# Linear attention into a snake MLP on one core: the order of the opening's loads, casts and copies, and of the second batch's preparation

## The chip, the cores and the metric

The kernel runs on one NeuronCore of a Trainium2 chip. The metric is the device time of one execution in microseconds (us). Five engines work side by side, each in its own program order: TensorE (PE, with its weight loads as PEld), VectorE (DVE), ScalarE (ACT), GpSimd (POOL) and SyncE (SP). SP, ACT and POOL also issue DMA transfers, each on a queue of its own; POOL's transfers here also cast float32 to bfloat16 on the way.

## The reference

q, k and v are float32 of 8 batches x 8 heads x 576 tokens x 64. Then a two-layer network with a periodic activation works on the 4608 tokens of 512 channels:

```python
q_s = softmax of q over its 64 channels
k_s = softmax of k over the 576 tokens
kv  = einsum('bhsd,bhse->bhde', k_s, v)
x   = einsum('bhsd,bhde->bhse', q_s, kv)        # (batch, token) x (head, channel)
h   = x @ w_in                                   # 512 -> 2048
g   = h + sin(alpha * h)**2 / (alpha + 1e-9)     # alpha: one number per hidden column
out = g @ w_out                                  # 2048 -> 512
```

## The kernel before, in words

**Tiling.** The tokens are worked off in nine blocks t of 512. The hidden layer of a block is 16 *slots* ni of 128 columns; a slot is four matmuls (`mm_h`, L261) over the four 128-row blocks of w_in in the order 0, 2, 1, 3, then a sine on ACT (L267), a square on ACT, POOL or DVE (L269, L271, L273) and a combine on DVE into g (`combine`, L277). The output of a block is four column groups of 16 matmuls each (`mm_o`, L281). A batch of tokens is split by head pairs into two halves `ii` (0 and 1). For each half the kernel does: exp of q and k on ACT, the sums and the division of q on DVE and POOL, eight transposes of q on PE (L199), the k-v product on PE (`kv_mm`, 36 small matmuls, L172), its normalization on DVE (`kv_norm`, L182), and four matmuls of q with it (`attn_x`, L216). These give two of the four row blocks of xT: half 0 gives blocks 0 and 2, half 1 gives 1 and 3.

**What sets the order.** The schedule is written by hand: every engine executes its instructions in the order of the code, and `take(os, n)` puts the next n output matmuls of the block before between other steps of PE. Semaphore waits follow from the data. A DMA is issued when its queue's engine reaches it. To hold an issue back, the code puts a one-element copy ahead of it: `GP_CP(held, ...)` on POOL waits until a load has landed, and a `DVE_CP` of a zero into the target of a load makes SP wait until DVE has come that far.

**The opening.** SP loads halves of batch 0: q, k, q, v, k (L309). ACT's queue loads alpha as 16 rows of 128 (L311); PE transposes it with the identity (L327), and DVE copies it to `alpha_sb` and takes the reciprocal (L328, L329). POOL waits for k's first half (L338), issues v's second half in two parts and then w_in by columns: 0 to 255 for row blocks 0 and 2, the same columns for 1 and 3, and then 256 columns at a time for all four row blocks up to 1023, later 512 at a time (L107), then w_out's first eight blocks of 128 rows (L110). DVE and POOL cast the two parts of v's second half (L335). xT of half 0 and the transposed q of half 1 are copied out of PSUM by DVE and ACT (L395 to L397); ACT loads its sine table at L398. PE then does the first two row blocks of slots 0 and 1, the attention matmuls of half 1, and the first two row blocks of slots 2 and 3. xT of half 1 is copied twice by DVE (L407).

**Block 0 and batch 1.** During the slots of block 0, the table `late` (L457) issues loads after certain slots: q of batch 1, first half, after slot 6; w_out blocks 8 to 11 after slot 8 and 12 to 13 after slot 10, on POOL; q's second half and all of k and v of batch 1 after slot 13, on SP. In the output of block 0 (`o_quad`) hidden blocks 12 to 15 come last: matmuls 49 to 56 need blocks 12 and 13, the last eight need 14 and 15. 46 output matmuls are followed by the steps of batch 1 with output matmuls between them (L486 to L512). POOL issues w_out blocks 14 and 15 once k of batch 1 has landed (L471, L472).

Of the kernel before, what the change touches and what calls it, by code (L numbers as in the profile page):

```python
# [23 lines left out]
def kernel(  # L24
# [14 lines left out]
    nc = tc.nc  # L39
# [7 lines left out]
    nN = d_ff // 128  # L47
# [58 lines left out]
    def load_win(c0, c1, cc=slice(0, 4)):  # L106
        nc.gpsimd.dma_start(out=win[:, cc, c0:c1], in_=win_v[:, cc, c0:c1])  # L107

    def load_wout(n0, n1):
        nc.gpsimd.dma_start(out=wout[:, n0:n1, :], in_=wout_v[:, n0:n1, :])  # L110


    A = {}
# [48 lines left out]
    def kv_mm(b, ii, pool, split=False):  # L162

        if ii == 0 or split:
            A["kvp", b] = pool.tile([128, 2, 512], F32, name="kvp", tag="a")
        kvp, ke, vt = A["kvp", b], A["ke", b], vb[b % 2]
        for j in range(J):
            for x in range(2):
                h = 2 * ii + x
                for e in range(2):  # L170
                    r = slice(64 * e, 64 * e + 64)
                    nc.tensor.matmul(kvp[64 * x:64 * x + 64, e, ii * 65:(ii + 1) * 65],  # L172
                                     ke[r, j, h * 64:(h + 1) * 64],
                                     vt[r, j, h * 65:(h + 1) * 65],
                                     start=(j == 0), stop=(j == J - 1))

    def kv_norm(b, i0=0, i1=2):

        kt, m = kbd[b % 2], i1 - i0
        kvr = small.tile([128, 2, 2], F32, name="kvr")[:, :, 0:m]  # L180
        src = A["kvp", b][:, :, i0 * 65:i1 * 65].rearrange("p e (ii c) -> p e ii c", ii=m)
        nc.vector.reciprocal(kvr, src[:, :, :, D])  # L182
        nc.vector.tensor_tensor(kt[:, :, i0:i1], src[:, :, :, 0:D],
                                kvr.unsqueeze(3).to_broadcast([128, 2, m, D]), op=ALU.mult)
# [123 lines left out]

    for n, t, ii in (("q", q, 0), ("k", k, 0), ("q", q, 1), ("v", v, 0), ("k", k, 1)):  # L309
        load0(nc.sync, n, t, ii, 0, 8 if n == "q" else J)  # L310
    nc.scalar.dma_start(out=alpha_rows, in_=moe_alpha.rearrange("(no ni) -> no ni", ni=128))  # L311
    make_identity(nc, ident)
    DVE_CP(identb, ident)
    zero = singles.tile([128, 1], F32, name="zero")
# [8 lines left out]

    tp0 = ps_h[0].tile([128, 8, 128], BF16, name="tp", tag="a")
    warm = ps_h[0].tile([128, 4, 128], F32, name="warm", tag="a")
    tpa = warm[:, 0, 0:nN]
    nc.tensor.transpose(tpa, alpha_rows, ident[0:nN, 0:nN])  # L327
    DVE_CP(alpha_sb, tpa)  # L328
    nc.vector.reciprocal(inva_sb, alpha_sb)  # L329

    def cast_v0(ii, j0, j1, eng):
        vv = vb[0].rearrange("p j (i c) -> p i j c", i=4)
        eng(vv[:, 2 * ii:2 * ii + 2, j0:j1, 0:D], staged["v", 0][:, ii::2, j0:j1])  # L335
# [2 lines left out]
    GP_CP(held, staged["k", 0][:, 0, 0, 0:1])  # L338
    load0(GP, "v", v, 1, 0, 5)
    load0(GP, "v", v, 1, 5, 9)  # L340
    for ii in range(2):
        load_win(0, 256, slice(ii, 4, 2))
    for c in range(1, 4):
        load_win(256 * c, 256 * c + 256)

    def warm_up(n):
# [36 lines left out]
    kv_norm(0, 0, 1)  # L383
    tp1 = ps_l.tile([128, 8, 128], BF16, name="tp", tag="l")
    q_transpose_ii(0, 1, 0, 8, tp1)
    cast_v0(1, 0, 5, DVE_CP)
    cast_v0(1, 5, 9, GP_CP)
    for c in range(2, 4):
        load_win(512 * c, 512 * c + 512)
# [2 lines left out]

    xp = [bank("b") for _ in range(2)]
    attn_x(0, 0, 0, 8, xp)
    DVE_CP(xT[:, 0, 0:MF], xp[0])  # L395
    ACT_CP(xT[:, 2, 0:MF], xp[1])
    ACT_CP(A["qT", 0][:, 1, 0:8], tp1)  # L397
    nc.scalar.activation(zero, zero, AX.Sin)  # L398
    kv_mm(0, 1, ps_k, split=True)
    kv_norm(0, 1, 2)  # L400
    for ki in range(2):
        for ni in range(2):
            mm_h(0, ni, ki, ki + 1)
    xp = [bank("l") for _ in range(2)]
    attn_x(0, 1, 0, 8, xp)
    for x in range(2):
        DVE_CP(xT[:, 2 * x + 1, 0:MF], xp[x])  # L407
    for ki in range(2):
        for ni in range(2, 4):
            mm_h(0, ni, ki, ki + 1)  # L410

    def h_slot(t, ni, sq, lag):
        hp = mm_h(t, ni, 2 if ni < (4, 1, 0)[min(t, 2)] else 0)
# [18 lines left out]
    def take(it, n=1000):  # L432
        for _ in range(n):
            if next(it, 0) == 0:
                return
# [4 lines left out]
    with ES:  # L440
        def load_q1(ii):
            if ii == 0:
                staged["q", 1] = stage.tile([128, 4, J, D], F32, name="st_q", tag="st")
            st = staged["q", 1]
            DVE_CP(st[:, ii, 0, 0:1], zero)
            nc.sync.dma_start(out=st[:, ii::2, 0:8].rearrange("p i j d -> p i (j d)"),
                              in_=src_view(q, 1)[:, ii::2, 0:8 * D])

        def load_kv1():
            for n in "kv":  # L450
                staged[n, 1] = stage.tile([128, 4, J, D], F32, name=f"st_{n}", tag="st")
            for ii in range(2):
                for n, t in (("k", k), ("v", v)):
                    nc.sync.dma_start(out=staged[n, 1][:, ii::2].rearrange("p i j d -> p i (j d)"),
                                      in_=src_view(t, 1)[:, ii::2])

        late = {6: lambda: load_q1(0), 8: lambda: load_wout(8, 12), 10: lambda: load_wout(12, 14), 13: lambda: (load_q1(1), load_kv1())}  # L457
        for ni in range(nN):
            h_slot(0, ni, "DPPAPPAPPAAPPAPD"[ni], lag)
            flush(lag, 1)  # L460
            if ni in late:
                late[ni]()
        flush(lag, 0)

        accs = [bank(kind) for kind in "bbll"]
        os = o_quad(0, accs, [DVE_CP, ACT_CP, DVE_CP, DVE_CP])
        take(os, 46)
        for ii in range(2):
            exp_half("q", 1, ii, 8)
        norm_q(1, [GP, V], 8)  # L470
        GP_CP(held, staged["k", 1][:, 0, 0, 0:1])  # L471
        load_wout(14, 16)  # L472

        def cast_v1(ii, eng):
            vv = vb[1].rearrange("p j (i c) -> p i j c", i=4)
            eng(vv[:, 2 * ii:2 * ii + 2, :, 0:D], staged["v", 1][:, ii::2])

        exp_half("k", 1, 0)
        cast_v1(0, ACT_CP)
        exp_half("k", 1, 1)  # L480
        def transpose_q1(ii):
            tp = ps_h[0].tile([128, 8, 128], BF16, name="tp", tag="a")
            q_transpose_ii(1, ii, 0, 8, tp)
            DVE_CP(q_tile(1)[:, ii, 0:8], tp)

        transpose_q1(0)  # L486
        take(os, 4)

        def x_half(ii):
            xp = [bank("a") for _ in range(2)]  # L490
            attn_x(1, ii, 0, 8, xp)
            for x in range(2):
                (ACT_CP, DVE_CP)[x](xT[:, 2 * x + ii, MF:2 * MF], xp[x])

        kv_mm(1, 0, ps_k, split=True)
        kv_norm(1, 0, 1)
        for b in range(2):
            DVE_CP(q8[:, 0, b, 0:1], zero)
            nc.sync.dma_start(out=q8[:, :, b], in_=src_view(q, b)[:, :, 8 * D:J * D])
        load_batch(2)  # L500
        cast_v1(1, DVE_CP)
        take(os, 4)
        x_half(0)
        take(os, 2)
        transpose_q1(1)
        kv_mm(1, 1, ps_k, split=True)
        kv_norm(1, 1, 2)
        take(os, 5)
        x_half(1)
        exp_to(A["qe", 1][:, J - 2:J], q8)  # L510
        nc.scalar.activation(zero, zero, AX.Sin)
        take(os)  # L512
        for ki in range(2):
            mm_h(1, 0, ki, ki + 1)
        norm_q8()
        load("q", q, 3)
        load("k", k, 3)
        load("v", v, 3)

        def late_q8(ni):  # L520
            if ni == 11:
                tp = ps_k.tile([128, 2, 2, 128], BF16, name="tp", tag="a")
                for b in range(2):
                    for ii in range(2):
                        nc.tensor.transpose(tp[:, ii, b], A["qe", 1][:, J - 2 + b, ii * 128:(ii + 1) * 128], identb)
                DVE_CP(A["qT", 1][:, :, J - 2:J], tp)
            elif ni == 15:
                xp = ps_k.tile([128, 2, 512], F32, name="xp", tag="a")
                for ii in range(2):
                    for b in range(2):  # L530
                        for e in range(2):
                            for x in range(2):
                                r, c = slice(64 * x, 64 * x + 64), (2 * ii + b) * P
                                nc.tensor.matmul(xp[64 * e:64 * e + 64, x, c:c + P], kbd[b][r, e, ii],
                                                 A["qT", 1][r, ii, J - 2 + b, e * 64:(e + 1) * 64],
                                                 start=True, stop=True)
                DVE_CP(xT[:, :, 16 * P:18 * P].rearrange("p (x i) n -> p x i n", x=2),
                       xp[:, :, 0:4 * P].rearrange("p x (i n) -> p x i n", i=2))

        for ni in range(nN):  # L540
            h_slot(1, ni, SQ[ni], lag)
            flush(lag, 1)
            late_q8(ni)
        cast_v(2, [GP_CP, GP_CP])
        flush(lag, 0)
# [149 lines left out]
```

## Time and profile before

| | |
|---|---|
| median of 3 runs | 283.48 us (283.33 to 284.21) |
| the profiled execution | 284.08 us, its span 282.3 us |
| PE busy | 267.7 us, 95% of the span |
| ACT, DVE, POOL busy | 223.7, 185.2, 81.8 us |
| granted TensorE clock | 0.999 |
| DMA | 45.82 MB; from 3 to 40 us the engines are about fully used |
| first output matmul of block 0 | 29.34 us |
| first matmul of block 1 | 46.46 us |

All times of day are us from the start of the span. A line of the timeline is: start, duration, engine, line of the code, operation, output tile <- input tiles with shapes, count, and in brackets the idle time of the engine before it and what ended it. Matmul durations overlap (0.379 us each while one starts every 0.216 us).

### The profile page before, as it was taken

The page shows a single profiled execution, that of the slowest core. Times are in us where ns is not written, and L with a number is a line of the kernel's source. Part 1 is how long each engine was busy: PE and PEld are TensorE (multiplying, and loading weights), DVE is VectorE, ACT ScalarE, POOL GpSimd, SP SyncE. Part 2 cuts the span into 40 slices and gives each one's busy share as a digit, 9 for nine tenths or more (in the row PEclk, how much of TensorE's full clock was granted, in tenths as well). Part 3 has the DMA queues.
Part 4 walks back from the last instruction along what each step waited for, and adds up shares of the span by engine and source line. Part 5 has one row for each costly group of instructions (what it writes and reads, how often), then busy time and mean ns, then how long its engine had stood idle before and what let it go on. Part 6 is the DMA issues. An engine that isn't in the chain of part 4 may idle for free.

```text
span 282.3 us, 4919 instructions
## 1 busy us (share of the span) xinstructions
PE 267.7 (95%) x1890; PEld 123.7 (44%) x1919; DVE 185.2 (66%) x280; ACT 223.7 (79%) x319; POOL 81.8 (29%) x76
## 2 busy tenths in 40 slices
PE   2789999999999999999999999999999999999994
PEld 1334444444444444444544444444444444444443
DVE  3858758799958767766775677667685555555412
ACT  4879666999588999899989998999877777777400
POOL 1868430777776550025003500341000000000000
PEclk9999999999999999999999999999999999999999
DMA  7999998996799129811992189125011111111143
GB/s 252 290 195 219 286 324 280 383 324 248 159 155 410 62 46 316 339 38 39 236 404 60 37 233 407 35 64 123 0 37 39 37 37 37 39 37 41 43 107 74
DMA packets 39048, 45.82 MB, mean 162 GB/s; under 512 B 16992, under 2 KB 22384, under 8 KB 39024
## 3 DMA queue, kind: packets, MB, share of 16 engines
q1 hardware_dynamic: 33360, 40.57, 46.9%
q0 software_dynamic: 5472, 4.79, 10.4%
q8 instruction: 15, 0.25, 0.4%
q10 hardware_dynamic: 192, 0.14, 0.2%
q14 instruction: 9, 0.07, 0.1%
HBM read 36.71 MB, written 9.44 MB: 163 GB/s over the span
## 4 chain that ended last, share of the span: by engine, by line
PE 85%; DMA 7%; POOL 3%; ACT 2%; issue 1%; DVE 1%; SPq 0%; ACTq 0%
PE op L281 38%; PE hp L261 37%; DMA st_v<-in_v_dram 3%; DMA win<-in_moe_w_in_dram 2%; PE kvp L172 2%; DMA st_k<-in_k_dram 2%; PE lp L261 2%; POOL s L271 1%; PE op L261 1%; PE op L665 1%; ACT s L267 1%; PE hp L216 1%; PE kvp L261 1%; PE xp L216 1%; POOL st_v L306 1%
## 5 line engine op out<-in xcount | busy, mean ns | idle before, releaser
L277 DVE SCALAR_TENSOR_TENSOR g<-s,inva_sb,hp 128x512 bf16<-128x512 f32 x128 | 94.5, 745 | 58.8 <-ACT s L269 53.3
L261 PE MATMUL hp<-xT,win 128*128 128x512 bf16 x505 | 127.5, 379 | 1.3 <-DMA win<-in_moe_w_in_dram 0.9
L281 PE MATMUL op<-wout,g 128*128 128x512 bf16 x478 | 121.0, 379 | 1.6 <-issue 1.1
L267 ACT ACTIVATE s<-hp,alpha_sb 128x512 f32<-128x512 f32 x128 | 86.2, 682 | 24.2 <-PE hp L261 22.9
L261 PEld LDWEIGHTS <-win 128*128 128x128 bf16 x576 | 55.8, 98 | 68.6 <-DMA win<-in_moe_w_in_dram 1.8
L281 PEld LDWEIGHTS <-g 128*128 128x128 bf16 x560 | 53.2, 98 | 64.7 <-issue 2.3
L269 ACT ACTIVATE s<-s 128x512 f32<-128x512 f32 x112 | 70.5, 630 | 3.6
L271 POOL TENSOR_TENSOR s<-s 128x512 f32<-128x512 f32 x29 | 30.1, 1055 | 22.6 <-ACT s L267 22.6
L151 POOL TENSOR_TENSOR qn<-qe,qs 128x1152 bf16<-128x1152 bf16 (+1 forms) x12 | 25.1, 2111 | 33.9 <-DVE qs L145 25.2
L293 DVE COPY o<-op 128x512 f32<-128x512 f32 (+2 forms) x33 | 21.8, 660 | 10.2 <-PE op L281 7.9
L136 POOL CAST vb<-st_v 128x1152 bf16<-128x1152 f32 x12 | 14.7, 1258 | 44.8 <-DMA st_v<-in_v_dram 44.8
L117 ACT ACTIVATE qe<-st_q 128x1152 bf16<-128x1152 f32 (+2 forms) x18 | 17.7, 1025 | 7.0 <-DMA st_q<-in_q_dram 6.9
L117 ACT ACTIVATE ke<-st_k 128x1152 bf16<-128x1152 f32 x16 | 17.9, 1151 | 0.9 <-DMA st_k<-in_k_dram 0.9
L144 DVE TENSOR_REDUCE qs<-qe 128x36 f32<-128x2304 bf16 x5 | 12.8, 2550 | 8.3 <-ACT qe L117 8.3
L117 ACT ACT_TABLE_LOAD x7 | 9.0, 1283 | 1.3 <-PEq L679 1.2
L281 PE MATMUL hp<-wout,g 128*128 128x512 bf16 x31 | 8.8, 379 | 0.1
L281 PE MATMUL lp<-wout,g 128*128 128x512 bf16 x30 | 8.6, 380 | 0.2 <-issue 0.2
L172 PE MATMUL kvp<-vb,ke 64*64 64x65 bf16 x576 | 6.9, 194 | 1.9 <-ACT vb L335 1.2
L172 PEld LDWEIGHTS <-ke 64*64 64x64 bf16 x576 | 5.9, 106 | 5.7 <-issue 3.0
L261 PE MATMUL lp<-xT,win 128*128 128x512 bf16 x31 | 7.5, 379 | 0.1
L229 DVE CAST xT<-xp 128x1024 bf16<-128x1024 f32 (+1 forms) x7 | 7.4, 1065 | 0.0
L149 DVE TENSOR_REDUCE qs<-qe 128x16 f32<-128x1024 bf16 (+1 forms) x4 | 5.1, 1266 | 3.4 <-ACT qe L117 3.4
(87 smaller groups left out, 131.8 us busy)
## 6 DMA issues: line engine op xcount, KB each, us to landing
out_dram<-o SPq DMA_DIRECT2D x70, 128.0 KB, 2.4
st_q<-in_q_dram SPq DMA_DIRECT2D x6, 1152.0 KB, 6.3
st_k<-in_k_dram SPq DMA_DIRECT2D x6, 1152.0 KB, 8.5
st_v<-in_v_dram SPq DMA_DIRECT2D x6, 1152.0 KB, 11.2
st_k<-in_k_dram SPq DMA_DIRECT2D x4, 576.0 KB, 7.7
st_q<-in_q_dram SPq DMA_DIRECT2D x4, 512.0 KB, 6.3
st_v<-in_v_dram SPq DMA_DIRECT2D x3, 576.0 KB, 8.2
wout<-in_moe_w_out_dram POOLq DMA_DIRECT2D x3, 512.0 KB, 12.5
```

What stands on the lines that cost most here:

```text
L117: nc.scalar.activation(dst[:, :, ii * 128:(ii + 1) * 128].rearrange("p j (x d) -> p x j d", x=2), src[:, ii::2], AX.Exp)
L136: engs[ii](vv[:, 2 * ii:2 * ii + 2, :, 0:D], staged["v", b][:, ii::2])
L144: nc.vector.tensor_reduce(qs, A["qe", b].rearrange("p j (i d) -> p j i d", i=4), axis=AXL.X, op=ALU.add)
L151: engs[ii % len(engs)].tensor_tensor(qn[:, ii, 0:j1].rearrange("p j (x d) -> p j x d", x=2), qe[:, ii], part.unsqueeze(3).to_broadcast([12 ...
L172: nc.tensor.matmul(kvp[64 * x:64 * x + 64, e, ii * 65:(ii + 1) * 65], ke[r, j, h * 64:(h + 1) * 64], vt[r, j, h * 65:(h + 1) * 65], start= ...
L261: nc.tensor.matmul(hp, win[:, KO[k], ni * 128:(ni + 1) * 128], xT[:, KO[k], t * MF % NX:t * MF % NX + MF], start=(k == 0), stop=(k == 3))
L267: nc.scalar.activation(s, hp, AX.Sin, scale=alpha_sb[:, ni:ni + 1])
L269: nc.scalar.activation(s, s, AX.Square)
L271: nc.gpsimd.tensor_tensor(s, s, s, op=ALU.mult)
L277: nc.vector.scalar_tensor_tensor(G[t][:, ni], in0=s, scalar=inva_sb[:, ni:ni + 1], in1=hp, op0=ALU.mult, op1=ALU.add)
L281: nc.tensor.matmul(acc, G[t][:, ni, j * 128:(j + 1) * 128], wout[:, ni, :], start=(ni == 0), stop=(ni == nN - 1))
L293: eng(o[:, cols], acc)
```

## The change

It has three parts.

- *Opening.* SP issues alpha as its sixth load. Its transpose, copy and reciprocal come after batch 0's second k-v product; the transpose goes to a free corner of that product's PSUM tile. w_in comes in other pieces: columns 0 to 255 and then 256 to 511 for row blocks 0 and 2, then columns 0 to 511 for row blocks 1 and 3, then as before. POOL casts both parts of v's second half. The transposed q of half 1 is copied by DVE, and both pairs of xT copies are shared by ACT and DVE. PE does three of the first eight hidden matmuls ahead of half 1's attention matmuls and five behind.
- *Batch 1's loads.* q, k and v are all issued after slot 11. w_out blocks 12 and 13 are issued by POOL after the exp of batch 1's q, behind a held copy that waits for q's second half.
- *Batch 1's steps.* Both groups of eight transposes come ahead of the first k-v product, with two output matmuls behind each; three, three and five more stand between the later steps. v's second half is cast by POOL.

```diff
     for n, t, ii in (("q", q, 0), ("k", k, 0), ("q", q, 1), ("v", v, 0), ("k", k, 1)):
         load0(nc.sync, n, t, ii, 0, 8 if n == "q" else J)
-    nc.scalar.dma_start(out=alpha_rows, in_=moe_alpha.rearrange("(no ni) -> no ni", ni=128))
+    nc.sync.dma_start(out=alpha_rows, in_=moe_alpha.rearrange("(no ni) -> no ni", ni=128))
...
-    tpa = warm[:, 0, 0:nN]
-    nc.tensor.transpose(tpa, alpha_rows, ident[0:nN, 0:nN])
-    DVE_CP(alpha_sb, tpa)
-    nc.vector.reciprocal(inva_sb, alpha_sb)
...
-    for ii in range(2):
-        load_win(0, 256, slice(ii, 4, 2))
-    for c in range(1, 4):
+    for c in range(2):
+        load_win(256 * c, 256 * c + 256, slice(0, 4, 2))
+    load_win(0, 512, slice(1, 4, 2))
+    for c in range(2, 4):
         load_win(256 * c, 256 * c + 256)
...
     q_transpose_ii(0, 1, 0, 8, tp1)
-    cast_v0(1, 0, 5, DVE_CP)
+    DVE_CP(A["qT", 0][:, 1, 0:8], tp1)
+    cast_v0(1, 0, 5, GP_CP)
     cast_v0(1, 5, 9, GP_CP)
...
     attn_x(0, 0, 0, 8, xp)
-    DVE_CP(xT[:, 0, 0:MF], xp[0])
-    ACT_CP(xT[:, 2, 0:MF], xp[1])
-    ACT_CP(A["qT", 0][:, 1, 0:8], tp1)
+    for x in range(2):
+        (ACT_CP, DVE_CP)[x](xT[:, 2 * x, 0:MF], xp[x])
     nc.scalar.activation(zero, zero, AX.Sin)
     kv_mm(0, 1, ps_k, split=True)
+    tpa = A["kvp", 0][:, 0, 256:256 + nN]
+    nc.tensor.transpose(tpa, alpha_rows, ident[0:nN, 0:nN])
     kv_norm(0, 1, 2)
-    for ki in range(2):
-        for ni in range(2):
-            mm_h(0, ni, ki, ki + 1)
+    DVE_CP(alpha_sb, tpa)
+    nc.vector.reciprocal(inva_sb, alpha_sb)
+    for ni, ki in ((0, 0), (1, 0), (0, 1)):
+        mm_h(0, ni, ki, ki + 1)
     xp = [bank("l") for _ in range(2)]
     attn_x(0, 1, 0, 8, xp)
     for x in range(2):
-        DVE_CP(xT[:, 2 * x + 1, 0:MF], xp[x])
-    for ki in range(2):
-        for ni in range(2, 4):
-            mm_h(0, ni, ki, ki + 1)
+        (ACT_CP, DVE_CP)[x](xT[:, 2 * x + 1, 0:MF], xp[x])
+    for ni, ki in ((1, 1), (2, 0), (2, 1), (3, 0), (3, 1)):
+        mm_h(0, ni, ki, ki + 1)
...
-        late = {6: lambda: load_q1(0), 8: lambda: load_wout(8, 12), 10: lambda: load_wout(12, 14), 13: lambda: (load_q1(1), load_kv1())}
+        late = {8: lambda: load_wout(8, 12), 11: lambda: (load_q1(0), load_q1(1), load_kv1())}
...
         for ii in range(2):
             exp_half("q", 1, ii, 8)
+        GP_CP(held, staged["q", 1][:, 1, 0, 0:1])
+        load_wout(12, 14)
         norm_q(1, [GP, V], 8)
...
         exp_half("k", 1, 1)
+        cast_v1(1, GP_CP)
...
-        transpose_q1(0)
-        take(os, 4)
...
+        for ii in range(2):
+            transpose_q1(ii)
+            take(os, 2)
         kv_mm(1, 0, ps_k, split=True)
         kv_norm(1, 0, 1)
...
         load_batch(2)
-        cast_v1(1, DVE_CP)
-        take(os, 4)
+        take(os, 3)
         x_half(0)
-        take(os, 2)
-        transpose_q1(1)
+        take(os, 3)
         kv_mm(1, 1, ps_k, split=True)
         kv_norm(1, 1, 2)
         take(os, 5)
```

## The prediction, made before the change was run

> **What bounds the kernel now.** I read the span by stages first (busy time of each engine in each stretch), since the page's averages mix stages. Columns: stretch, its length, then busy us and instructions of PE, PEld, DVE, ACT, POOL, the granted clock, the DMA share, GB/s.
>
> ```profile
> 16.10:29.30 13.20, 13.05 (x59) 5.81 (x61) 9.67 (x15) 11.50 (x20) 9.60 (x11) 1.00 1.25 222
> 29.30:46.40 17.10, 16.57 (x158) 7.94 (x160) 12.23 (x24) 9.71 (x13) 4.26 (x5) 1.00 0.98 276
> 46.40:61.10 14.70, 14.61 (x86) 6.67 (x85) 12.48 (x21) 13.87 (x25) 9.35 (x9) 1.00 0.99 353
> ```
>
> From 16.1 us on TensorE is the bound: 13.05 of 13.20 us, then 16.57 of 17.10, then 14.61 of 14.70, and 215.68 of the last 221.2. After 46.4 nothing is touched and the engine is full, so what the change does to the moment of 46.46, the first matmul of block 1, it does to the end. There are two places where PE can gain or lose: the opening, and batch 1's steps between 29.3 and 46.4. Note the DMA shares near or above 1: from 3 to 40 us the transfers are saturated.
>
> The timeline of the opening:
>
> ```profile
> 14.80 0.41 PE L216 MATMUL lp<-qT,kbd 64*64 64x512 bf16 x4
> ...
> 16.11 2.76 PE L261 MATMUL hp<-xT,win 128*128 128x512 bf16 x12 [0.91 <-DMA win<-in_moe_w_in_dram]
> ...
> 22.41 6.59 PEld L261 LDWEIGHTS <-win 128*128 128x128 bf16 x32 [0.58 <-DMA win<-in_moe_w_in_dram]
> ```
>
> PE stands 0.91 us until 16.11 for w_in's columns 256 to 511, and once more near 22.4 for columns 1024 on. TensorE's timeline over batch 1's steps:
>
> ```profile
> 39.26 0.61 PE L199 MATMUL tp<-identb,qn 128*128 128x128 bf16 x8
> ...
> 40.86 0.48 PE L172 MATMUL kvp<-vb,ke 64*64 64x65 bf16 x36
> 41.50 0.38 PE L281 MATMUL lp<-wout,g 128*128 128x512 bf16 x1 [0.16 <-issue]
> ...
> 43.33 0.61 PE L199 MATMUL tp<-identb,qn 128*128 128x128 bf16 x8
> 43.87 0.48 PE L172 MATMUL kvp<-vb,ke 64*64 64x65 bf16 x36
> ...
> 46.46 0.81 PE L261 MATMUL kvp<-xT,win 128*128 128x512 bf16 x3
> ```
>
> The 46 output matmuls from 29.34 to 39.26 give 9.92/46 = 0.216 us each. From 41.50 to 46.46 PE does 14 of them (3.02), two groups of attention matmuls (0.41 each), eight transposes (0.54) and a kv product (0.45): 4.83 of 4.96 us, hardly a stall. What is left to win here is about 0.3 us, ahead of 40.86.
>
> Then the DMA view, window by window: SP's queue at 38 to 40 us with a POOL transfer issued in it; v's last half; POOL's queue at 12 to 15 and at 18 to 21 us (packets, MB, share).
>
> ```profile
> q1 hardware_dynamic: 351, 0.76, 97.8%
> ...
> wout<-in_moe_w_out_dram POOLq DMA_DIRECT2D x1, 256.0 KB, 5.3
> ```
>
> ```profile
> st_v<-in_v_dram SPq DMA_DIRECT2D x1, 576.0 KB, 10.0
> ```
>
> ```profile
> q0 software_dynamic: 929, 0.46, 129.6%
> ```
>
> ```profile
> q0 software_dynamic: 624, 0.61, 124.4%
> ```
>
> POOL issued w_out's blocks 14 and 15 at 38.50 and they landed at 43.8. The last v half was issued at 32.47 and landed at 42.47. At 208 packets per us (624 in 3 us), the 256 packets of that w_out transfer take 1.23 us: it landed just that long after v. So it went behind everything that SP had queued, not between.
>
> **The change: the opening.** The alpha transpose moves from 3.8 us, where PE was idle, to behind the kv product that ends at 13.90. Its row is 0.25 us. Three hidden matmuls (0.65) bring PE to 14.8, the attention matmuls start at about 14.9 (before 14.80) and end at 15.3. Their copies, one after the other on DVE before (15.25 to 16.54), now run on ACT (0.59) and DVE (0.69) together: done at 16.0. Meanwhile five matmuls (1.08) need only w_in's columns 256 to 511 of row blocks 0 and 2, which now come second instead of with the third transfer. PE reaches slot 0 at 16.4; before it was 16.11 + 4 x 0.216 = 16.97. That is 0.55 us.
>
> Costed at nothing, with its cover: alpha as SP's sixth load lands after k's second half (issued 2.88, 8.1 us to land: 11.0) and is wanted at 13.9, so 2.5 us would have to go wrong; it is SP's last, so nothing is behind it until 24 us. DVE's alpha copy and reciprocal (0.18 + 0.25) fit its idle 0.81 before 15.25. The q copy on DVE (0.68 by the same copy at 40.58, ACT took 1.02) runs 12.36 to 13.04, and xT from 13.04 to 13.73; kv_norm starts at 13.95 as before. ACT loads its sine table earlier. POOL's extra cast (0.62 x 640/512 = 0.78) fits between 11.93 and 12.74; its next cast waits for v until 12.90 anyway.
>
> w_in: 512 packets of 512 B become 256 of 1 KB. POOL's queue moved 340 of the small ones per us at 14 to 15 us (929 in 3 us on average, 386 at 16 to 17) and 208 of the large: 512/340 - 256/208 = 0.28 us sooner for all later weights (bounds 0.10 and 0.42). Columns 1024 on then release PE at 22.13 instead of 22.41, but PE now wants them at 16.4 + 24 x 0.216 = 21.6. So 0.5 us of wait opens there, and of the 0.55 only 0.28 is kept: the first output matmul comes at 29.06 instead of 29.34.
>
> **The change: batch 1.** All of q, k, v are issued by SP at slot 11, behind a DVE copy that follows the tenth combine (28.03 before, 27.75 now): from 28.05 to 30.7, where before q's first half went at 24.27 and the rest at 30.52 to 33.0. w_out's blocks 12 and 13, issued by POOL at about 26.6 before, now wait on POOL for q's second half. PE's steps from 29.06: 46 matmuls (9.92) to 38.98, eight transposes (0.45) to 39.43, two matmuls to 39.86, eight transposes (0.57) to 40.4. The next two are for hidden block 12 and need those blocks.
>
> When do they land? The engines are saturated and the bytes the same, so I count back from the end of the busy stretch. It ended with v at 42.47; 0.28 less for the packets gives 42.2. Now w_out 12 and 13 come last: 1.23 before that, at 40.95, v's second half; k, v, k and q go before it in steps of 1.43 (39.62, 41.05, 42.47 in the rows of before): k 39.5, v 38.1, k 36.7, q 35.25. POOL's held copy (0.19) lets it issue at 35.45. First packets came 2.4 us after issue at 6.61 and 1.8 at 38.50, so at 37.3 to 37.9, when k's and v's second halves stand in the queue. By the row above it goes behind them: 42.2. Bounds: 35.45 + 5.3, the shortest of this size, 40.75; and 42.2 + 0.8 = 43.0 if SP's first packets come late (issue at 24.27, first seen in the half us from 27.0) and the engines run dry after w_out's blocks 8 to 11. I take 42.2, for the nearest row is a w_out transfer of the same size behind the same loads.
>
> The Trainium skill speaks otherwise: "DMA: Bandwidth & Descriptors", section "Queues, rings and completion order", says that each engine takes turns between the queues that have work, packet by packet. By it w_out would share at once and land near the lower bound, and the sum would be 283.2; this trace's row of 38.50 does not agree.
>
> The sum: 42.2; two matmuls, 42.63; the kv product up to the next matmul (40.86 to 41.50), 43.27; then the stretch that took 4.96 before, less the 0.54 of transposes moved ahead: 47.69, against 46.46. That is 1.2 us later. Queued behind PE's wait are the kv product, kv_norm, q8's loads and batch 2's (SP), all later by the same. What else moves is covered: q exp, sums and norm end at about 39.2 (DVE) and 38.4 (POOL), before the transposes want them; v's cast on POOL (1.26 for DVE's 0.76) ends by 42.3, wanted at 44.5; w_out 14 and 15, 1.23 behind 42.2, wanted at 45.3.
>
> The profiled execution took 284.08 (span 282.3, 1.8 around it), 0.6 above the median of 283.48; I add the difference to the median: 284.7.
>
> **The rivals.**
> 1. *w_out 12 and 13 get a share at once* (not slower). For it: POOL's queue is separate. Against: 38.50. At 40.75 PE waits 0.35; end 40.75 + 5.49 = 46.24: 283.2. It decides for the change from a landing before 41.0.
> 2. *No wait at all, and w_in early too.* PE keeps 0.55 from the opening and loses the 0.3 ahead of 40.86: 282.6 (faster by 0.3%). It needs w_in 0.5 us and w_out 1.8 us sooner than saturated engines gave.
> 3. *Only some engines are late.* At 40 to 41 us SP's share is 29.7% and POOL's 51.6%: most engines had finished. If w_out waits only for these, 41.2: +0.2, 283.7.
> 4. *The engines run dry at 30 us*: landing 43.0, 285.5.
> 5. *The change doesn't do what it says*: alpha's lateness or the extra POOL casts hold PE at 13.9. Each is covered by 0.2 to 2.5 us; part of case 3.
>
> **How the numbers follow.** Forecast (284.4 to 285.1) 0.41; rival 4 0.07; rival 1 0.15; rival 3 with 5 0.11; rival 2 0.26, given room since its two conditions are both landing times, which no row fixes within 0.5 us. 0.3% is 0.85 us, about what a measurement of this kernel can tell from no change. Slower 0.41 + 0.07 = 0.48, same 0.15 + 0.11 = 0.26, faster 0.26. The range, 282.5 to 285.2, leaves out half of rival 4 and about a half of rival 2's tail; since cases of both signs hold weight, the forecast's own is 284.4 to 285.1.
>
> **What would show it.** Right: PE reaches slot 0 near 16.4 and waits for w_in near 22; the first output matmul near 29.1; one PE wait of 1 to 2 us, released by DMA wout, after the second eight transposes; first matmul of block 1 near 47.7. Wrong: no PE wait near 40.4 (rivals 1, 2), or POOL packets among SP's at 37.5 to 40.

## The result and the profile after

The changed kernel took 285.70 us (284.83 to 285.89, 6 runs); the kernel before took 283.40 (6 runs). The ratio is 1.0079, 95% interval 1.0057 to 1.0102: slower by 2.3 us, where 1.2 was forecast. The range given ended at 285.2. The profiled execution took 285.79 us, its span 284.0. Ratios, here and below, leave out a few slow executions and are not the quotients of the medians, so the two can differ by some tenths of a per cent.

Busy time by stages of the changed kernel (columns as above). The stages are cut at its own first slot, its first output matmul and its first matmul of block 1:

```profile
15.60:28.00 12.40, 12.33 (x55) 5.29 (x57) 9.30 (x15) 11.53 (x20) 8.56 (x9) 1.00 1.25 201
28.00:48.20 20.20, 17.66 (x158) 8.13 (x160) 12.25 (x22) 9.69 (x12) 7.23 (x8) 0.92 0.90 262
48.20:62.80 14.60, 14.55 (x86) 6.62 (x84) 12.46 (x21) 13.87 (x25) 9.33 (x9) 1.00 0.98 353
```

The middle stage holds the loss: 20.2 us where it was 17.1, and its mean granted clock is 0.92. The stages before and after it are as full as they were, and from the first matmul of block 1 to the end every profile of this case takes 235.7 to 236.0 us, so what the moment of block 1 loses, the end loses. TensorE's timeline in the middle stage:

```profile
37.96 0.61 PE L199 MATMUL tp<-identb,qn 128*128 128x128 bf16 x8
38.41 0.59 PE L281 MATMUL lp<-wout,g 128*128 128x512 bf16 x2
38.84 0.61 PE L199 MATMUL tp<-identb,qn 128*128 128x128 bf16 x8
41.46 0.84 PE L281 MATMUL hp<-wout,g 128*128 128x512 bf16 x2 [2.01 <-DMA wout<-in_moe_w_out_dram]
42.23 0.71 PE L172 MATMUL kvp<-vb,ke 64*64 64x65 bf16 x36
43.27 0.63 PE L281 MATMUL lp<-wout,g 128*128 128x512 bf16 x1 [0.33 <-issue]
43.70 0.63 PE L281 MATMUL hp<-wout,g 128*128 128x512 bf16 x1
44.27 0.64 PE L216 MATMUL hp<-qT,kbd 64*64 64x512 bf16 x4
...
48.29 1.03 PE L261 MATMUL kvp<-xT,win 128*128 128x512 bf16 x4
```

The wait is where it was forecast, behind the second eight transposes and for w_out, 2.01 us long. But what comes after it is slow as well: single output matmuls take 0.63 us in place of 0.38, and they start 0.43 us apart in place of 0.216. The stages microsecond by microsecond tell why; the granted clock is the third number from the end:

```profile
40.00:41.00 1.00, 0.00 (x0) 0.00 (x0) 0.18 (x1) 0.00 (x0) 0.40 (x1) 1.00 1.06 156
41.00:42.00 1.00, 0.54 (x2) 0.10 (x1) 0.00 (x0) 0.00 (x0) 0.77 (x1) 0.83 0.75 116
42.00:43.00 1.00, 0.94 (x37) 0.70 (x38) 0.01 (x1) 0.00 (x0) 0.00 (x0) 0.50 0.13 22
43.00:44.00 1.00, 0.72 (x2) 0.15 (x1) 0.57 (x4) 0.00 (x0) 0.00 (x0) 0.50 0.00 0
44.00:45.00 1.00, 1.00 (x6) 0.27 (x6) 0.01 (x1) 0.05 (x1) 0.00 (x0) 0.50 0.24 57
45.00:46.00 1.00, 1.00 (x39) 0.41 (x37) 0.68 (x1) 0.54 (x1) 0.00 (x0) 0.96 1.07 211
```

Half speed from about 41.66 to 45.08: 0.34 us of the second microsecond, three whole ones and 0.08, together 3.4 us. The profile before has 1.00 throughout. In five of the six executions the mean clock of the span was 0.994; in the one with 1.0 the time was 284.83, the shortest.

The Trainium skill, "TensorE: Matmul & The Clock Gate", section "Part 1: The HAM clock gate", says that the array falls to half its clock after an idle window of about 3.4 us, and that the windows run freely. The half speed and the 3.4 us agree with the trace; but here 2.0 us without a matmul were enough in the profiled execution, so the gap need not be as long as the window.

The DMA view at 34 to 36 us, for POOL's issue at 34.49 (transfer, size, us to landing), and POOL's timeline, which shows when v's second half was there:

```profile
wout<-in_moe_w_out_dram POOLq DMA_DIRECT2D x1, 256.0 KB, 6.9
```

```profile
34.49 0.77 POOL L110 DMA_DIRECT2D wout<-in_moe_w_out_dram  x1 [0.27 <-issue]
...
40.60 1.16 POOL L477 CAST vb<-st_v 128x1152 bf16<-128x1152 f32 x1 [1.41 <-DMA st_v<-in_v_dram]
```

34.49 + 6.9 is 41.4: w_out's blocks 12 and 13 came 0.8 us after v's second half, which released POOL just ahead of 40.60. The queues at 36 to 38 us and at 38 to 40 us (q1 is SP's, q0 POOL's; packets, MB, share):

```profile
q1 hardware_dynamic: 367, 0.79, 100.9%
```

```profile
q0 software_dynamic: 236, 0.23, 71.1%
q1 hardware_dynamic: 125, 0.26, 35.6%
```

From 34.49 to 38 us POOL's queue moved no packet at all; its first came near 38.1, 3.6 us after the issue.

In the opening, PE reached slot 0 at 15.59 and the first output matmul came at 28.03, where the profile before had 16.97 and 29.34. The experiments show that less than this is the change's doing.

### The profile page after: what moved, and what is told of

Same layout as the page of the kernel before. It is cut to its first block, busy times and chain, and to the rows that moved or that the text cites. A ratio compares the mean times of both kernels' runs of the same rounds, so it can differ in the third digit from the quotient of the medians.

```text
span 284.0 us, 4922 instructions
## 1 busy us (share of the span) xinstructions
PE 270.0 (95%) x1890; PEld 124.3 (44%) x1919; DVE 184.9 (65%) x278; ACT 223.4 (79%) x319; POOL 84.7 (30%) x79
## 4 chain that ended last, share of the span: by engine, by line
PE 85%; DMA 9%; POOL 2%; issue 1%; DVE 1%; ACT 1%; SPq 0%; POOLq 0%
PE op L281 38%; PE hp L261 37%; DMA wout<-in_moe_w_out_dram 2%; DMA st_q<-in_q_dram 2%; DMA win<-in_moe_w_in_dram 2%; PE kvp L172 2%; DMA st_k<-in_k_dram 2%; PE lp L261 2%; PE op L261 1%; PE op L666 1%; PE hp L216 1%; PE hp L281 1%; PE kvp L261 1%; ACT s L267 1%; DVE g L277 1%
## 5 line engine op out<-in xcount | busy, mean ns | idle before, releaser
L136 POOL CAST vb<-st_v 128x1152 bf16<-128x1152 f32 x12 | 14.7, 1257 | 44.3 <-DMA st_v<-in_v_dram 29.1
L281 PE MATMUL hp<-wout,g 128*128 128x512 bf16 x32 | 9.7, 400 | 2.1 <-DMA wout<-in_moe_w_out_dram 2.0
L346 PE MATMUL warm<-qe,identb 128*128 128x512 bf16 x10 | 4.7, 619 | 5.2 <-ACT qe L117 5.2
```

The lines of the kernel that those rows point to most:

```text
L136: engs[ii](vv[:, 2 * ii:2 * ii + 2, :, 0:D], staged["v", b][:, ii::2])
L281: nc.tensor.matmul(acc, G[t][:, ni, j * 128:(j + 1) * 128], wout[:, ni, :], start=(ni == 0), stop=(ni == nN - 1))
```

## The experiments

Theory: the loss is PE's wait for w_out blocks 12 and 13, which land behind the loads that SP has queued, and the slow clock that follows from the wait; the opening gives a little back. Rivals: the new steps or the late q, k and v cost it; it is the faster opening that makes the wait; the clock has no part. The medians of before on the chips of the three sets were 282.85, 282.79 and 282.96 us.

**The kernel before, once more.** No edit.

> The kernel before, unchanged, profiled a second time. In its first profile batch 0's loads reached two of the sixteen DMA engines 0.65 us late and v's first half landed at 9.5 us; in the changed kernel at 8.65. Theory A (alpha's early transfer, beside q's first packets, delays them): ACT's cast of v starts again at 9.4 to 9.6. Theory B (chance of one execution): it starts somewhere else, 8.7 to 9.2.

The cast started at 8.76, as in theory B, and the first output matmul came at 28.78, not 29.34. So 0.6 us of the difference at the first output matmul in the first pair of profiles is chance of one execution. This one took 283.96 us, the first profile 284.08: both lie above the medians of before.

**Alpha alone.**

```diff
-    nc.scalar.dma_start(out=alpha_rows, ...)       # issued on ACT's queue, transposed at the start
+    nc.sync.dma_start(out=alpha_rows, ...)         # SP's sixth, transposed after kv_mm(0, 1)
```

> The kernel before with the alpha part alone: alpha sixth on SP's queue, its transpose after the second k-v product. Theory A: loads land 0.5 to 0.85 us earlier and the first output matmul comes 0.5 to 0.8 us earlier; the end too, 282.6 to 282.9 if before stands at 283.4. Theory B: only the 0.25 us of the transpose moves, into the wait for w_in; within 0.2 us of before.

282.49 against 282.85, ratio 0.9985 (0.9960 to 1.0009): no difference that is resolved. Its one profile has the first output matmul at 27.69, 1.1 us ahead of the second profile of before, though v landed at the same time (8.72 and 8.76): the third piece of w_in came at 14.7 in place of 15.8. The medians do not bear out a whole us, and theory A's reason (alpha's early transfer makes v late) is refuted by the run before it. What moved w_in in the one profile stays open.

**The whole opening, batch 1 as before.**

> The whole opening part (alpha, w_in's pieces, casts, copies, the order of the first eight hidden matmuls) with the loads and steps of batch 1 as before. Theory: the opening gives 1.3 us at the first output matmul (28.03 as in the changed kernel) and there is no wait for w_out, so the end comes 0.8 to 1.3 us earlier than before, 282.1 to 282.6. Rival (the gain of the opening is given back where k and v of batch 1 land): within 0.4 us of before.

282.56, ratio 0.9980 (0.9953 to 1.0006); first output matmul at 27.79, no wait for w_out, block 1 at 44.89. The gain is at most small: the middle of the interval is 0.6 us, the difference of the medians 0.3. The forecast's 0.28 fits; the 1.3 us of the two profiles lies at the very edge of the interval.

**Batch 1's part alone, the opening as before.**

> The part on batch 1 alone (its loads at slot 11, w_out blocks 12 and 13 behind q's second half, the new order of steps), with the opening as before. Theory (w_out's late landing): PE waits 1.5 to 2.5 us for w_out near 41 us, the clock is granted at half speed for some 3.4 us after it in most executions, and the end comes 2 to 3.5 us later than before. Rival (it is the earlier PE of the new opening that makes the wait, since w_out would be in time for the old one): a wait under 0.7 us and within 0.5 us of before.

286.41, ratio 1.0106 (1.0075 to 1.0137). Its line on PE:

```profile
42.59 0.59 PE L281 MATMUL hp<-wout,g 128*128 128x512 bf16 x2 [2.58 <-DMA wout<-in_moe_w_out_dram]
```

```profile
47.96 1.03 PE L261 MATMUL kvp<-xT,win 128*128 128x512 bf16 x4
```

So the wait is not made by a faster opening: with the old one it was 2.58 us. In six of its ten executions the mean clock was 0.993 or 0.994, in the others about 1.0, the profiled one among them. It gives the price at full clock: from the first matmul after the wait to block 1 it took 5.37 us, where the changed kernel at half clock took 6.83 for the same steps.

**w_out blocks 12 and 13 after slot 10 again, all else as changed.**

```diff
-        late = {8: ..load_wout(8, 12), 11: ..(load_q1(0), load_q1(1), load_kv1())}
+        late = {8: ..load_wout(8, 12), 10: ..load_wout(12, 14), 11: ..(load_q1(0), load_q1(1), load_kv1())}
-        GP_CP(held, staged["q", 1][:, 1, 0, 0:1])
-        load_wout(12, 14)
```

> The changed kernel with w_out blocks 12 and 13 issued after slot 10 again, without the held copy; everything else as changed. Theory (w_out queued behind SP's loads is the whole loss): no PE wait for w_out, PE's clock stays at full speed, first matmul of block 1 at 44.5 to 45.5, and the time 0.3 to 1.0 us under before. Rival (the loads at slot 11 and the new order of steps cost something too, q, k and v landing 1.2 us later behind w_out): a new wait for q or v of 0.5 us or more, and the time at or above before.

283.94, ratio 1.0041 (1.0018 to 1.0064): by the ratio better than the changed kernel, though the two intervals just overlap, and slower than before. The rival is right here. No PE wait for blocks 12 and 13 is left, but q's halves, now behind them, reach ACT at 34.72, and PE waits for the division of q:

```profile
39.46 0.62 PE L199 MATMUL tp<-identb,qn 128*128 128x128 bf16 x8 [1.90 <-POOL qn L151]
```

**The held copy away, POOL issues at once.**

```diff
-        GP_CP(held, staged["q", 1][:, 1, 0, 0:1])
         load_wout(12, 14)
```

> The changed kernel without the held copy alone: POOL issues w_out blocks 12 and 13 as soon as it is through with block 0's squares, near 29.8 us instead of 34.5, when q's halves, k and v have all been issued by SP. Theory (a POOL transfer goes behind the SP packets that already stand in the engines' queues, some 30 each, and not behind all that SP has issued): it lands at 36 to 38.5, PE doesn't wait, time within 0.5 us of the kernel with the issue after slot 10. Rival (it goes behind all that SP has issued): it lands near 41.4 again, PE waits 2 us as in the changed kernel.

283.41, ratio 1.0020 (0.9993 to 1.0047), not told apart from before, and 0.5 us under the kernel with the issue after slot 10. POOL issued at 29.32, and w_out landed 8.3 us later, at 37.6. SP had issued k and v between 27.29 and 29.45. The first half of k was there at 36.28 and that of v at 39.33 (27.93 + 11.4): w_out came between, ahead of three transfers that SP had issued earlier. So POOL's transfer neither goes behind everything that SP has issued, nor does it take turns from the start; it goes behind a stretch of it. Its first packets came near 33.3, 4.0 us after the issue; from then on the two queues did take turns, as at 34 to 36 us:

```profile
q1 hardware_dynamic: 186, 0.41, 58.8%
q0 software_dynamic: 180, 0.18, 54.0%
```

What takes the place of the wait is v: its first half reached ACT at 39.37, 2.5 us later than in the changed kernel (36.84), of which w_out's own packets are some 1.2:

```profile
40.59 0.48 PE L172 MATMUL kvp<-vb,ke 64*64 64x65 bf16 x36 [1.06 <-ACT vb L476]
```

**Second halves of k and v held back, so that less stands in front of w_out.**

```diff
-        late = {..., 11: ..(load_q1(0), load_q1(1), load_kv1())}
+        late = {..., 11: ..(load_q1(0), load_q1(1), load_kv1(0))}
         norm_q(1, [GP, V], 8)
+        load_kv1(1)        # behind a DVE copy of a zero into k's tile
```

> The changed kernel with the second halves of batch 1's k and v issued later on SP, behind a DVE copy after q's division (near 38.5 us), so that they do not stand in the queues when POOL issues w_out blocks 12 and 13. Theory (w_out lands when what stands ahead of it is through): it lands two steps of 1.43 us earlier, 38.3 to 39.3, and PE doesn't wait for it; PE waits instead for v's second half, by 1 to 3 us, since that lands at 43 or later. Rival (a POOL transfer needs 6.9 us on its own): it lands near 41.4 as before.

One execution only, 289.72 us. w_out was issued at 35.27 and landed in 4.2 us, at 39.5, in time for PE; the view of its issue:

```profile
wout<-in_moe_w_out_dram POOLq DMA_DIRECT2D x1, 256.0 KB, 4.2
```

6.9 us with k's and v's second halves in the queues, 4.2 without: the rival (6.9 us on its own) is refuted, and the difference fits what stood in front. PE then waited 4.67 us for POOL's cast of v, longer than expected, since the second halves were issued only at 39.28 and 39.70; and the clock fell again (0.50 from 45.8 to 52.6 us).

**Nine matmuls in the wait.** They write a PSUM tile that nobody reads.

```diff
             transpose_q1(ii)
+            if ii == 1:
+                keep = ps_k.tile([128, 2, 512], F32, name="kvp", tag="a")
+                for _ in range(9):
+                    nc.tensor.matmul(keep[:, 0], identb, xT[:, 0, 0:MF], start=True, stop=True)
             take(os, 2)
```

> The changed kernel with nine added matmuls of 128x512 on PE after the second eight transposes, into a PSUM tile that nobody reads: 9 x 0.216 = 1.9 us of work where PE stood for 2.0. It adds work and leaves nothing out. Theory (the wait also lets the clock fall to half speed for 3.4 us): the wait for w_out shrinks to a few tenths, the clock stays at 1.0 at 41 to 45 us, first matmul of block 1 at 46.9 to 47.2 instead of 48.29, and the median is 0.7 to 1.3 us under that of the changed kernel, still above before. Rival (the slow clock has no part in it): the same time as the changed kernel or later.

284.66, ratio 1.0067 (1.0043 to 1.0091), too near the changed kernel's interval to settle it across sets. So both ran again on one chip:

> The changed kernel as it is, once more, beside the one with nine added matmuls on the same chip. The wait for w_out near 41 us again, 1.7 to 2.6 us; where the granted clock falls to half the first matmul of block 1 comes at 48 to 48.5, where it does not at 47 to 47.5. Median 285.0 to 285.6 with before at 282.8.

> The changed kernel with nine added matmuls of 128x512 after the second eight transposes, as before, now beside the changed kernel. They leave nothing out. Theory (the wait makes the clock fall in most executions): clock 1.0 in all executions, and the median 0.4 to 1.0 us under the changed kernel's of the same chip. Rival: no difference over 0.2 us.

The changed kernel: 286.62, ratio 1.0106 (1.0066 to 1.0146), mean clock 0.988 to 0.994 in all six executions, the wait 2.58 us, block 1 at 48.74. With the nine matmuls: 284.72, ratio 1.0050 (1.0024 to 1.0077), the clock 0.998 to 1.0 in all twelve, block 1 at 46.69. The changed kernel's median lies above the 285.6 expected. Added work made it 1.9 us faster by the medians, 1.6 by the ratios, more than the 1.0 expected; the intervals overlap a little, but five of the six times lie above all twelve of the other kernel, and the profiles show the mechanism. The changed kernel in the microseconds after its wait, then the other one in the same stretch:

```profile
42.00:43.00 1.00, 1.00 (x30) 0.38 (x33) 0.00 (x0) 0.00 (x0) 0.73 (x1) 0.59 0.13 20
43.00:44.00 1.00, 0.67 (x29) 0.48 (x19) 0.57 (x4) 0.00 (x0) 0.00 (x0) 0.50 0.00 0
44.00:45.00 1.00, 1.00 (x6) 0.13 (x4) 0.01 (x1) 0.00 (x0) 0.00 (x0) 0.50 0.00 0
```

```profile
42.00:45.00 3.00, 2.84 (x84) 1.36 (x78) 1.60 (x7) 0.58 (x1) 0.00 (x0) 1.00 0.26 59
```

PE is called busy in both; only the clock, here 0.50 to 0.59 against 1.00, tells them apart. The kernel with the nine matmuls takes, from the first matmul that needs blocks 12 and 13 to block 1:

```profile
41.32 0.59 PE L281 MATMUL hp<-wout,g 128*128 128x512 bf16 x2
...
46.69 1.03 PE L261 MATMUL kvp<-xT,win 128*128 128x512 bf16 x4
```

That is 5.37 us again, where both profiles of the changed kernel have 6.83 (41.46 to 48.29, 41.91 to 48.74). The clock is thus worth 1.46 us; the other 0.59 between these two profiles is w_out, which PE could use at 41.32 in one and at 41.91 in the other, a difference that the nine matmuls do not explain.

**The new steps with the old loads.** The opening and the order of steps as changed, all loads after slots 6, 10 and 13.

> The changed kernel with all loads of batch 1 and w_out blocks 12 and 13 issued where they were before (slots 6, 10, 13); the opening and the new order of steps stay. Theory (both the late w_out and the late q, k and v come from the loads; the steps alone add only one wait, since the second transposes want q's second half 3 us earlier than before): one PE wait of 0.5 to 1.5 us before the second eight transposes, none for w_out, 283.0 to 284.0 with before at 282.8. Rival (the steps are harmless): within 0.3 us of the opening alone, 282.6.

282.71, ratio 0.9989 (0.9962 to 1.0016). The rival is right: the steps are harmless. The second transposes wait 0.42 us for q, and block 1 begins at 45.23. So the whole loss is in when the loads are issued.

None of these kernels is faster than before by more than its interval.

## Why the prediction was wrong

**The term that failed.** "The sum: 42.2; two matmuls, 42.63; the kv product ..., 43.27; then the stretch that took 4.96 before": 5.49 us from the landing to block 1, priced at the rows of before, at full clock. The changed kernel took 6.83 (41.46 to 48.29). The wait was forecast and its consequence for the clock left out: half speed for 3.4 us. At full clock the stretch was priced rightly, for it took 5.37 in the two profiles named above; the half clock adds 1.46. With it the forecast would have been 2.7 us slower; measured were 2.3 and, the second time, 3.7 by the medians (0.8% and 1.1% by the ratios). In the pair of profiles another error works against it: PE could go on at 41.46, 0.7 us earlier than forecast, so that block 1 came 0.6 us late (48.29 for 47.69), not 1.3. The rivals had the same hole: none of them could give more than rival 4's 285.5, and its own reason, engines running dry at 30 us, is not what happened (the DMA share was 1.04 to 1.19 at 29 to 32 us).

**The start of the sum.** The difference was taken from a profile with block 1 at 46.46 and added to the median. By the 235.8 us from there to the end and the 1.8 around the span, the median of 283.40 has block 1 near 45.8 (an estimate): the profiled execution was late by 0.7. A kernel that is held by w_out's landing need not share that. It would account for most of the distance between the 2.3 us of the medians and the 1.83 of the profiles, but no run shows it by itself.

**The wait.** Place and releaser were right. PE wanted w_out at 39.45 (40.4 forecast), it landed at 41.4 (42.2), the wait was 2.01 (1.8). Both ends came almost 1 us early, so the errors cancel, and the length of the wait is right partly by luck. That one reason, the earlier opening of that execution, moved both is likely but not shown: in the second execution PE was there at 39.33 and w_out only at 41.9.

**Who goes first.** The step "it goes behind them", taken from one row, gave the right order in the changed kernel, where w_out landed after v, and a landing 0.8 us too late. As a general statement it was too strong: issued at 29.32, w_out overtook three earlier transfers. The row of 38.50 could not carry it either, since few of SP's packets were left when POOL's came (59 beside 67 at 40 to 41 us). The first packets were forecast 1.8 to 2.4 us after the issue; they came after 3.6 and 4.0 us with SP's loads in the queues. The rule of turns by packet that the prediction cites from the Trainium skill ("DMA: Bandwidth & Descriptors", section "Queues, rings and completion order") does not fit that stretch, in which POOL's queue moved nothing; it fits what follows, 186 packets of SP beside 180 of POOL. A picture that fits all the rows is that the engines hold a stock of SP's packets that a later transfer cannot pass. How large it is was not measured.

**The opening.** 0.28 us was forecast and the opening alone measured 0.3 by the medians, not resolved. PE's waits for later columns of w_in came, but near 19 and 21 and together 0.3 to 0.5 us long in the profiles of the changed kernel and of the opening alone, where one of 0.5 near 22 was forecast.

**What was costed at nothing.** POOL's casts, the q copy on DVE, alpha and the order of steps were covered, as the run with the old loads shows. The later q, k and v were not: they were hidden only by the wait for w_out. Once that is gone, the division of q (1.90 us) or v (1.06) is next, and the kernel stays 1.2 or 0.6 us slower than before by the medians, the second not resolved. The prediction did not say what was late next.

**The rivals.** Rival 1 (a share at once) and rival 2 (no wait) are refuted by the wait; rival 3's 41.2 came near the landing, but PE was early too. Its reason holds in part: by the traces' semaphore records fourteen of w_out's sixteen parts had landed by 40.62 and the last at 41.42, in the second execution fifteen by 40.92 and the last at 41.87. Rival 5 is refuted by the run with the old loads.

## What to carry to other kernels

A wait of TensorE is priced with the clock that comes back after it: here a wait of 2 us cost another 1.5, and filling it with idle matmuls took that back. A load that is moved late in a stretch where the DMA engines are saturated lands behind what already stands in front of it (6.9 us here, 4.2 with less in front), so count back from the end of the busy stretch, in bytes, and ask for each consumer which load is now last. Two profiles of one kernel may differ by over half a us in the opening (28.78 and 29.34 here); take the size of a small gain from medians.

## What was not expected of the hardware

Gaps of 2.0 and 2.6 us without a matmul were followed by half clock for 3.4 us in the two profiles of the changed kernel; by the mean clock it fell in eleven of its twelve executions, and in six of ten of the kernel with batch 1's part alone. The kernel before has a low clock at times too: in six of its 81 executions beside these runs the mean was 0.992 to 0.994, and they took 285.2 to 286.5 us; where in them the clock fell was not profiled.

Which gaps do it can be read from the traces' clock records. Within a trace the changes lie whole steps of 3.413 us apart: in the changed kernel half clock from 41.66 to 45.08 is one step, with the held-back halves from 45.81 to 52.64 two. Laid on these steps, gaps with 2.01, 2.57 and 3.26 us inside one step were followed by half clock from the step's end (the changed kernel twice, the held-back halves). Gaps with 1.79 us inside one step were not (the kernel before once more, w_out after slot 10), nor was the 2.58 us gap of batch 1's part alone, which the end of a step at 41.26 divides into 1.26 and 1.32. This fits every profile here, but no run moved a gap along the steps by itself.

A 256 KB transfer of POOL took 4.2, 5.3, 6.9 or 8.3 us to land in the runs above, by what stood in front of it.
